# A Mamba-2 scan and a GELU layer on one core: a new order of steps, with the decay products pe on GpSimd and seven filler units fewer

## The chip, the cores and the metric

The kernel runs on one core of a Trainium2 chip. The core has five engines with an instruction queue each: TensorE (PE in the profile; its weight loads are listed as PEld), VectorE (DVE), ScalarE (ACT), GpSimd (POOL) and SyncE (SP), which here only issues DMA transfers. An engine runs its queue strictly in order, so an instruction that waits holds up all that stand behind it. The engines wait for each other by semaphores. The metric is the device time of one launch in microseconds, the median of several runs.

## The reference

The first half is a chunked state-space scan. For each of 4 batches and 8 heads, with 768 tokens of 32 values (x), 16 state values (B, C) and a decay a per token, and with cum the running sum of log a within a chunk:

```python
CB = np.einsum('bhin,bhjn->bhij', Cc, Bc)
M = CB * L                                   # L = exp(cum_i - cum_j), causal
y_intra = np.einsum('bhij,bhjd->bhid', M, xc)
y_inter = np.einsum('bhin,bhnd->bhid', Cc, state) * decay_to_i[:, :, :, None]
y[:, :, sl] = y_intra + y_inter
Bx = np.einsum('bhjn,bhjd->bhjnd', Bc, xc) * decay_from_j[:, :, :, None, None]
state = decay_full[:, :, None, None] * state + np.sum(Bx, axis=2)
```

The second half takes y as 3072 tokens of 256 values through two matrices, `w_in` (256 x 2048) and `w_out` (2048 x 256):

```python
h = x @ w_in
g = 0.5 * h * (1.0 + np.tanh(c * (h + 0.044715 * h * h * h)))
return (g @ w_out).astype(np.float32)
```

## The kernel before, in words

The kernel's chunks have 128 tokens, so a batch has 6. Two chunks of a batch are a unit, and there are 12 units, 0 to 11; units 0 to 2 are batch 0, 3 to 5 batch 1, 6 to 8 batch 2, 9 to 11 batch 3. The work is cut into named steps. A name ends in the unit, chunk or batch that it works on.

**Decays.** `clip` and `R` make running products of a on VectorE; `tp2`, `tp6` turn them and `recip` inverts them. `pe` multiplies the first element of each chunk's clipped a by its running product and spreads the result over a mask, two small products of 128 x 3 and 128 x 48 (L419, L420). `pp` multiplies that on TensorE with a selection matrix, and `pend` copies the result out: the decay of each whole chunk.

**B and C of a batch.** `load_bc.b.i` fetches them (i = 0 is B, 1 is C); `mul.b.i` scales them by the decays into the tile bc16. For batch 1 they are turned on TensorE (`T`, `N`). For batches 2 and 3 they go by way of DRAM: `load_wr.b.i` (L524) writes bc16 to a scratch tensor scr, `load_tr.b.i` (L531) reads it back with a DMA transpose, as ch from C and as bh from B, and `load_bn.b` (L536) reads scr of B once more untransposed. `F.b` (L549) makes ce from ch on VectorE.

**A unit of the scan.** `load_x.u` and `castx.u` bring x of the unit as bf16. `G.u` forms the products of C and B into two PSUM tiles ga, gb (L637, L644); it needs bh and ce of its batch. `M.u.0` and `M.u.1` mask them on VectorE (L654, 1024 columns each). `D.u` forms the state's increment (L679), `S.u.k` updates the state (L750, L752), `SP.c` makes the masked and decayed state of a chunk for the next one (L759). `Y.u` adds up the output; from unit 4 on it is `Yi.u` for the part within chunks (L721) and `YI.u` for the part from the state (L734), and `yev` or `yew` copies it to the tile xm (L348 on ScalarE, L352 on VectorE, L350 on GpSimd: the lines of one helper, `copy`).

**The GELU layer.** `s1.u.i` multiplies `w_in` with xm (units 0 to 3: L790, eight steps of four matmuls; later L795, sixteen steps of two matmuls with 512 columns for two units together, named after the even one). `gelu.u.i` follows on ScalarE (L801, L804). `s2.u.k.q` multiplies with `w_out` (L816, four matmuls), `oev` copies the result out and `store` writes it. `wi` and `wo` cast the weights. All of `s1` and most of `D` and `pp` take turns in the PSUM banks a, b, o and y; a step that takes a bank waits until the bank's last content was copied out.

**Order.** Nothing is scheduled at run time. The string ORDERED lists all steps; the kernel calls them from left to right, and each step appends its instructions to the queue of its engine. So the place of two steps in the string sets their order only if they share an engine. `:A`, `:D`, `:P`, `:S` behind a name pick the engine for steps that may run on several, `@b` picks the PSUM bank. `~51` is filler: matmuls of zeros into bank y, in units of 128 columns, up to four units a matmul (L773).

```python
    def fill(t, n):
        w3 = wz.rearrange("p (o t) -> p o t", o=1)
        for k in range(0, n, 4):
            m = min(4, n - k)
            nc.tensor.matmul(out=t[:, 0:m * 128], lhsT=wz, rhs=w3.to_broadcast([128, m, 128]),
                             start=True, stop=True, skip_group_check=True)
```

Of the kernel before, what the change touches and what calls it, by code (L numbers as in the profile page):

```python
# [11 lines left out]
ALU = mybir.AluOpType  # L12
# [7 lines left out]
c_m16 mulc.0 ~51 tw.1 ew.1.1:A mulc.1 tw.2 mulb c_sub c_unp c_ends ~4 tw.0 peq ew.0.2 ew.0.1 load_wi.1  # L20
ew.0.0:A ew.1.2 c_par ~4 G.0 x4.1 ew.1.0 x4.0:D M.0.0 ~4 ppq GE.2 GE.3 pendq XX.0 ME.2 XD.0 xn.1 ME.3
xn.0:D load_wi.2 SP.0 ~17 Y.0 wi.0.1:A wi.0.0:A S.0.0 clip R S.0.1 yev.0.0.2 wi.1.1 XX.1 XD.1 wi.1.0 tp2
wi.2.1 xn.2 s1.0.0 G.1 S.1.0 s1.0.1 xn.3 gelu.0.0 gelu.0.1 s1.0.2 gelu.0.2 M.1.1 wi.2.0 M.1.0 s1.0.3
gelu.0.3 s1.0.4 s1.0.5 recip1 S.1.1 gelu.0.4 gelu.0.5 SP.1 load_wi.3 wi.3.1 wi.3.0 load_bc1.1 s1.0.6
load_bc1.0 mul1.0:P SP.2 pe mul1.1:P T1.0 bh1:D tp6 Y.1 gelu.0.6 pp load_wo.0 pend:D yev.1.0.2 T1.1 N1
wo.0.0 s1.0.7 load_x.2 ce1.1:D castx.2.None ce1.0:D recip.1 s1.1.0 bn1 SP.3 gelu.0.7 wo.0.1 G.2 D.2
gelu.1.0 S.2.0 s1.1.1 gelu.1.1 s2.0.0.0 s1.1.2 gelu.1.2 s1.1.3 load_bc.1.1 SP.4 load_bc.1.0 M.2.1 M.2.0
gelu.1.3 load_wo.1 s2.0.1.0 mul.1.0 s1.1.4 hold.4 mul.1.1:P recip.2 load_x.3 gelu.1.4 wo.1.0 s1.1.5
wo.1.1 Y.2 gelu.1.5 castx.3.None s1.1.6 yev.2.0.2 T.1.0 s1.1.7 gelu.1.6 load_wo.2 E.1.0 T.1.1 s1.2.0 N.1
gelu.1.7 gelu.2.0 E.1.1 bn.1:D s1.2.1 F.1 s2.0.0.1 wo.2.0 wo.2.1:D s1.2.2 gelu.2.1 s2.0.1.1 D.3 G.3 S.3.0  # L30
gelu.2.2 s1.2.3 gelu.2.3 S.3.1 M.3.0 M.3.1 load_wo.3 load_x.4 wo.3.0:A s2.0.0.2 s2.0.1.2 wo.3.1 SP.6
s1.2.4 s1.2.5 castx.4.None s2.0.0.3 s2.0.1.3 gelu.2.4 gelu.2.5 oev.0:D s1.2.6 load_bc.2.1 load_bc.2.0
# [50 lines left out]
def kernel(  # L83
# [10 lines left out]
    nc = tc.nc  # L94
# [988 lines left out]
```

## Time and profile before

| what | value |
|---|---|
| median of three runs | 116.25 us (115.82 to 116.44) |
| the profiled execution | 115.84 us, span 114.1 us |
| TensorE busy | 107.5 us (94% of the span) |
| VectorE, ScalarE, GpSimd busy | 68.1, 69.7, 24.7 us |
| share of the chain that ended last | PE 78%, SP's queue 9%, DMA 7% |
| filler matmuls (L773) | 21, 7.6 us busy |

The span runs from the first to the last instruction; what the execution takes beyond it, 1.7 us, lies around it. Times in the views are counted from the span's start. The chain is followed back from the last instruction, at each step to what released it, so a share in it says what set the end. A matmul's length in the timeline holds its way through the array: two that follow each other overlap, and their distance is told by their starts. "x4" means that a row stands for four instructions. The engine of a DMA's issue is written SPq; its length there is that of the issue, and the landing is told apart.

### The profile page before, as it was taken

The page shows a single profiled execution, that of the slowest core. Times are in us where ns is not written, and L with a number is a line of the kernel's source. Part 1 is how long each engine was busy: PE and PEld are TensorE (multiplying, and loading weights), DVE is VectorE, ACT ScalarE, POOL GpSimd, SP SyncE. Part 2 cuts the span into 40 slices and gives each one's busy share as a digit, 9 for nine tenths or more (in the row PEclk, how much of TensorE's full clock was granted, in tenths as well). Part 3 has the DMA queues.
Part 4 walks back from the last instruction along what each step waited for, and adds up shares of the span by engine and source line. Part 5 has one row for each costly group of instructions (what it writes and reads, how often), then busy time and mean ns, then how long its engine had stood idle before and what let it go on. Part 6 is the DMA issues. An engine that isn't in the chain of part 4 may idle for free.

```text
span 114.1 us, 3122 instructions
## 1 busy us (share of the span) xinstructions
PE 107.5 (94%) x1277; PEld 77.6 (68%) x1285; DVE 68.1 (60%) x136; ACT 69.7 (61%) x135; POOL 24.7 (22%) x53
## 2 busy tenths in 40 slices
PE   6998889999999999999999999999999999999990
PEld 2345566888879888665677765777657776777870
DVE  4789999999989597798509704658444411020110
ACT  3149688687673727479666778725865666654400
POOL 6635676736319000130200200000000000000000
PEclk9999999999999999999999999999999999999999
DMA  0999989989998768968777502220000023201032
GB/s 24 243 303 306 353 222 203 311 151 345 207 215 136 158 163 188 294 128 195 185 161 142 116 0 96 97 92 6 0 0 0 6 91 116 69 0 52 0 138 92
DMA packets 43102, 15.99 MB, mean 140 GB/s; under 512 B 36688, under 2 KB 41552, under 8 KB 43088
## 3 DMA queue, kind: packets, MB, share of 16 engines
q1 hardware_dynamic: 42896, 15.70, 54.9%
q8 instruction: 10, 0.16, 0.7%
q10 hardware_dynamic: 192, 0.09, 0.3%
q14 instruction: 4, 0.03, 0.1%
HBM read 11.07 MB, written 3.93 MB: 131 GB/s over the span
## 4 chain that ended last, share of the span: by engine, by line
PE 78%; SPq 9%; DMA 7%; ACT 1%; issue 1%; POOL 1%; DVE 0%; POOLq 0%
PE bank_o L816 19%; PE bank_y L816 16%; PE bank_b L795 10%; PE bank_a L795 7%; PE bank_b L790 5%; PE bank_a L790 4%; SPq L154 4%; PE bank_o L795 4%; DMA bcf<-in_B_dram 4%; DMA x_t<-in_x_dram 3%; PE bank_y L795 3%; SPq L194 3%; PE bank_b L816 2%; PE bank_a L816 2%; PE ga L637 1%; PE bank_y L721 1%
## 5 line engine op out<-in xcount | busy, mean ns | idle before, releaser
L816 PEld LDWEIGHTS <-gT 128*128 128x128 bf16 x384 | 37.1, 98 | 10.4 <-issue 0.6
L816 PE MATMUL bank_o<-w_out_sb,gT 128*128 128x256 bf16 x192 | 26.1, 273 | 0.0
L816 PE MATMUL bank_y<-w_out_sb,gT 128*128 128x256 bf16 x160 | 21.2, 273 | 0.1
L795 PEld LDWEIGHTS <-w_in_sb 128*128 128x128 bf16 x128 | 14.1, 114 | 7.7 <-issue 0.4
L804 ACT ACTIVATE gT<-bank_b 128x512 bf16<-128x512 f32 x25 | 14.9, 598 | 6.6 <-PE bank_b L795 6.1
L654 DVE TENSOR_TENSOR m<-ga,tri 128x1024 bf16<-128x1024 f32 x12 | 14.6, 1216 | 5.3 <-PE gb L637 5.3
L804 ACT ACTIVATE gT<-bank_a 128x512 bf16<-128x512 f32 x21 | 12.6, 599 | 6.6 <-PE bank_a L795 2.5
L790 PEld LDWEIGHTS <-w_in_sb 128*128 128x128 bf16 x128 | 13.6, 113 | 2.3 <-issue 1.5
L795 PE MATMUL bank_b<-xm,w_in_sb 128*128 128x512 bf16 x48 | 14.5, 380 | 0.2
L801 ACT ACTIVATE gT<-bank_b 128x512 bf16<-128x512 f32 x17 | 10.1, 596 | 6.8 <-PE bank_b L790 6.7
L654 DVE TENSOR_TENSOR m<-gb,tri 128x1024 bf16<-128x1024 f32 x11 | 13.4, 1216 | 0.1
L352 DVE COPY o_sb<-bank_y 128x256 f32<-128x256 f32 x5 | 2.1, 424 | 15.7 <-PE bank_y L816 13.7
L795 PE MATMUL bank_a<-xm,w_in_sb 128*128 128x512 bf16 x36 | 11.2, 380 | 0.1
L801 ACT ACTIVATE gT<-bank_a 128x512 bf16<-128x512 f32 x15 | 8.9, 595 | 2.7 <-PE bank_a L790 2.6
L790 PE MATMUL bank_b<-xm,w_in_sb 128*128 128x256 bf16 x68 | 10.3, 273 | 0.2 <-DVE s_new L752 0.2
L790 PE MATMUL bank_a<-xm,w_in_sb 128*128 128x256 bf16 x60 | 9.0, 272 | 0.9 <-ACT gT L801 0.4
L759 DVE SCALAR_TENSOR_TENSOR sp_new<-s_new,pend,bmask 128x256 bf16<-128x256 f32 x17 | 9.4, 568 | 0.3 <-DVE s_new L752 0.2
L773 PE MATMUL bank_y<-wz 128*128 128x512 bf16 (+2 forms) x21 | 7.6, 512 | 1.1 <-DVE warm L225 1.1
L352 DVE CAST xm<-bank_a 128x512 bf16<-128x512 f32 x4 | 2.8, 692 | 9.0 <-PE bank_a L734 9.0
L804 ACT ACTIVATE gT<-bank_o 128x512 bf16<-128x512 f32 x10 | 6.0, 596 | 2.4 <-PE bank_o L795 2.3
L510 POOL TENSOR_TENSOR bc<-bc_t,pt 128x768 bf16<-128x768 f32 x3 | 4.5, 1494 | 13.0 <-DMA bc_t<-in_C_dram 10.7
L348 ACT ACTIVATE xm<-bank_y 128x512 bf16<-128x512 f32 x8 | 4.8, 594 | 3.6 <-PE bank_a L734 3.1
(149 smaller groups left out, 131.8 us busy)
## 6 DMA issues: line engine op xcount, KB each, us to landing
out_dram<-o_sb SPq DMA_DIRECT2D x24, 128.0 KB, 1.8
x_t<-in_x_dram SPq DMA_DIRECT2D x20, 128.0 KB, 4.3
wf<-in_moe_w_in_dram SPq DMA_DIRECT2D x4, 512.0 KB, 7.6
wf<-in_moe_w_out_dram SPq DMA_DIRECT2D x4, 512.0 KB, 6.0
bc_t<-in_C_dram SPq DMA_DIRECT2D x3, 384.0 KB, 4.7
bc_t<-in_B_dram SPq DMA_DIRECT2D x3, 384.0 KB, 6.0
scr<-bc SPq DMA_DIRECT2D x4, 192.0 KB, 2.7
x_t<-in_x_dram SPq DMA_DIRECT2D x1, 512.0 KB, 4.5
```

The costliest lines, as they stand in the source:

```text
L154: nc.sync.dma_start(out=BC0[1][:, i], in_=(B, C)[i][0, :, c * Q:(c + n) * Q, :] .rearrange("h (p r) n -> p h (r n)", r=n))
L348: nc.scalar.activation(o, i, AF.Copy)
L352: nc.vector.tensor_copy(out=o, in_=i)
L510: (nc.gpsimd if eng == "POOL" else nc.vector).tensor_tensor(out=d["bc16"][:, i], in0=d["bc"].rearrange("p i h (r n) -> p i r h n", r=R6)[: ...
L654: nc.vector.tensor_tensor(out=m_of(u)[:, 2 * i:2 * i + 2].rearrange("p g k e t -> p (g k e) t"), in0=gx[i].rearrange("p g (k t) -> p (g k) ...
L759: nc.vector.scalar_tensor_tensor(out=sp_new.rearrange("p (g d) -> p g d", g=4), in0=(XN[0][:, H * D:H * D + 64] if gc == 0 else state[("s" ...
L773: nc.tensor.matmul(out=t[:, 0:m * 128], lhsT=wz, rhs=w3.to_broadcast([128, m, 128]), start=True, stop=True, skip_group_check=True)
L790: nc.tensor.matmul(out=hp[:, j * T:(j + 1) * T], lhsT=w_in_k[:, w, q, k], rhs=xm[:, w, u * T:(u + 1) * T], start=(w == 0), stop=(w == 1))
L795: nc.tensor.matmul(out=hp, lhsT=w_in_k[:, w, q, k], rhs=xm[:, w, u * T:u * T + PT], start=(w == 0), stop=(w == 1))
L801: nc.scalar.activation(gts[u][:, 2 * i:2 * i + 2], hp.rearrange("p (j t) -> p j t", j=2), AF.Gelu_apprx_tanh)
L804: nc.scalar.activation(gts[("p", u)][:, i], hp, AF.Gelu_apprx_tanh)
L816: nc.tensor.matmul(out=ops[gc], lhsT=gts[u][:, fi, k * Q:(k + 1) * Q], rhs=w_out_sb[:, fi, :], start=(fi == 0 and (u > 0 or k == 0)), stop ...
```

## The change

There are three parts. The step `pe` takes an engine as argument and now runs on GpSimd; the first filler has 44 units in place of 51; and all steps from the transposed x of unit 1 (`XX.1`) on stand in a new order, some with another engine or bank. Up to there the order is the old one, but that `G.1` and `S.0.1` move into it and `clip` stands later.

```diff
-c_m16 mulc.0 ~51 tw.1 ew.1.1:A mulc.1 tw.2 mulb c_sub c_unp c_ends ~4 tw.0 peq ew.0.2 ew.0.1 load_wi.1
+c_m16 mulc.0 ~44 tw.1 ew.1.1:A mulc.1 tw.2 mulb c_sub c_unp c_ends ~4 tw.0 peq ew.0.2 ew.0.1 load_wi.1
...
-s2.4.0.3 oev.8:A F.3 s1.6.0@a gelu.6.0 s1.6.1@b SP.18 s1.6.2@o s2.4.1.0@y s2.4.1.1 gelu.6.1 s1.6.3@b
...
+s1.4.15@b s2.4.0.0@o M.7.1 s2.4.0.1 gelu.4.14 gelu.4.15 Yi.6@ya D.8@b D.9@y Yi.7 G.8 YI.6 YI.7 S.9.0
+S.9.1 castx.10.None:D yew.6.1 S.8.0 yew.6.0 s2.4.0.2 s2.4.0.3 oev.8:D s1.6.0@a s1.6.1@b gelu.6.1
...
-    def f_pe():
+    def f_pe(eng):
+        ve = nc.gpsimd if eng == "POOL" else nc.vector
         first = [t[:, 0:QL].rearrange("p (c t) -> p c t", t=Q // 2)[:, :, 0] for t in (ac, r_t)]
-        nc.vector.tensor_tensor(out=pe1, in0=first[0], in1=first[1], op=ALU.mult)
-        nc.vector.tensor_tensor(
+        ve.tensor_tensor(out=pe1, in0=first[0], in1=first[1], op=ALU.mult)
+        ve.tensor_tensor(
             out=pe2, in0=pe1.rearrange("p (o c) -> p o c", o=1).to_broadcast([128, 4 * batch, 3]),
             in1=m16.rearrange("p (j o) -> p j o", o=1).to_broadcast([128, 4 * batch, 3]), op=ALU.mult)
...
-    pe_ = add("D", f_pe, deps=[R, cm16])
+    pe_ = add("D", f_pe, alt="DP", deps=[R, cm16])
```

The old order had `Yi.6@ya Yi.7 D.8@b D.9 YI.6 YI.7 G.8 yew.6.1 yew.6.0 S.9.0 s2.4.0.2 S.8.0 S.9.1` ahead of the removed line shown second. Units 8 and 9 go the same way: G.10 stood behind YI.9 and now stands ahead of YI.8. At unit 10, `s2.8.0.2 s2.8.0.3 s2.8.1.0` stood between YI.11 and s1.10.0; now the first two do. Lines of the changed kernel stand one to two further down than those named above.

The first place is SP's queue around the scratch copies of batch 2. Here scr21 is the scratch of C, scr20 that of B; x_t_777 is x of unit 6, x_t_848 of unit 7, x_t_774 of unit 5. Before:

```order
L168 DMA bc_t_771<-in_C_dram 128x8x96
L168 DMA bc_t_771<-in_B_dram 128x8x96
L175 DMA x_t_774<-in_x_dram 128x8x32 x2
L175 DMA x_t_777<-in_x_dram 128x8x32 x2
L524 DMA scr21_842<-bc16_834 128x768
L175 DMA x_t_848<-in_x_dram 128x8x32 x2
L524 DMA scr20_852<-bc16_834 128x768
L531 DMA_TRANSPOSE ch_854<-scr21_842 128x768
L536 DMA bn_857<-scr20_852 128x6x128
L531 DMA_TRANSPOSE bh_865<-scr20_852 128x768
```

Now, with x of units 5, 6 and 7 as x_t_724, x_t_849 and x_t_859:

```order
L176 DMA x_t_724<-in_x_dram 128x8x32 x2
L169 DMA bc_t_750<-in_C_dram 128x8x96
L169 DMA bc_t_750<-in_B_dram 128x8x96
L176 DMA x_t_849<-in_x_dram 128x8x32 x2
L526 DMA scr20_857<-bc16_753 128x768
L176 DMA x_t_859<-in_x_dram 128x8x32 x2
L526 DMA scr21_866<-bc16_753 128x768
L533 DMA_TRANSPOSE ch_876<-scr21_866 128x768
L538 DMA bn_892<-scr20_857 128x6x128
L533 DMA_TRANSPOSE bh_910<-scr20_857 128x768
```

The two copies to scr have changed places, x of unit 5 has moved ahead of B and C of batch 2, and the two transposes stand as before. What the first copy waits for is on VectorE now, where mul.2.0 (bc16_753) follows both M.4 (m_840) and the cast of unit 5:

```order
L353 COPY o_sb_776<-bank_o_145 128x256
L754 SCALAR_TENSOR_TENSOR s_new_821<-s_new_707,pend_129,bank_b_144 128x64
L754 SCALAR_TENSOR_TENSOR s_new_831<-s_new_821,pend_129,bank_b_144 128x64
L353 CAST x16_834<-x_t_724 128x512
L656 TENSOR_TENSOR m_840<-gb_142,tri_112 128x1024
L656 TENSOR_TENSOR m_840<-ga_141,tri_112 128x1024
L512 TENSOR_TENSOR bc16_753<-bc_t_750,rt_126 128x768
```

Before, both products of batch 2 (bc16_834) stood on GpSimd, C's first:

```order
L350 CAST w_out_sb_139<-wf_650 128x512
L350 CAST w_out_sb_139<-wf_728 128x512
L350 CAST x16_753<-x_t_730 128x512
L510 TENSOR_TENSOR bc16_834<-bc_t_771,pt_127 128x768
L510 TENSOR_TENSOR bc16_834<-bc_t_771,rt_126 128x768
L510 TENSOR_TENSOR bc16_918<-bc_t_885,pt_127 128x768
```

C's product of batch 2 stayed there; B's left.

The second place is VectorE ahead of D.2. Before, from recip1 on:

```order
L408 RECIPROCAL pt01_125<-rt01_123 128x16
L752 SCALAR_TENSOR_TENSOR s_new_441<-s_new_409,pendq_128,bank_o_145 128x64
L759 SCALAR_TENSOR_TENSOR sp_new_445<-s_new_344,pendq_128,bmask_111 128x256
L759 SCALAR_TENSOR_TENSOR sp_new_458<-s_new_409,pendq_128,bmask_111 128x256
L419 TENSOR_TENSOR pe1_107<-ac_104,r_t_106 128x3
L420 TENSOR_TENSOR pe2_108<-pe1_107,m16_113 128x48
L352 COPY bh01_135<-ga_141 128x256
L375 STREAM_TRANSPOSE rt_126<-r_t_106 128x192
```

Now, from recip1 to the cast of unit 2 (x16_528):

```order
L409 RECIPROCAL pt01_125<-rt01_123 128x16
L472 TENSOR_TENSOR bc0s1_131<-bcf1_95,pt01_125 128x256
L353 CAST xm_140<-bank_y_146 128x2x2x128
L353 COPY bh01_135<-ga_141 128x256
L376 STREAM_TRANSPOSE rt_126<-r_t_106 128x192
L353 COPY pend_129<-bank_a_143 128x2x4x2
L353 COPY pend_129<-bank_a_143 128x2x4
L353 CAST w_out_sb_139<-wf_492 128x512
L353 CAST x16_528<-x_t_500 128x512
```

The two products of pe are gone from here, and mul1.1, yev.1, a cast of `w_out` and castx.2 have come.

The third place is VectorE at the evacuation of unit 6's xm (yew.6.1, the CAST of xm). Before:

```order
L654 TENSOR_TENSOR m_1205<-gb_142,tri_112 128x1024
L352 CAST xm_140<-bank_a_143 128x512
L750 COPY s_new_1318<-bank_b_144 128x64
L752 SCALAR_TENSOR_TENSOR s_new_1324<-s_new_1111,pend_129,bank_b_144 128x64
L752 SCALAR_TENSOR_TENSOR s_new_1326<-s_new_1318,pend_129,bank_b_144 128x64
```

Now:

```order
L656 TENSOR_TENSOR m_1193<-gb_142,tri_112 128x1024
L752 COPY s_new_1314<-bank_b_144 128x64
L754 SCALAR_TENSOR_TENSOR s_new_1316<-s_new_1314,pend_129,bank_b_144 128x64
L353 CAST x16_1318<-x_t_1130 128x512
L353 CAST xm_140<-bank_a_143 128x512
L754 SCALAR_TENSOR_TENSOR s_new_1321<-s_new_1109,pend_129,bank_b_144 128x64
```

Two updates of the state and the cast of x of unit 10 (x_t_1130) have moved ahead of the evacuation.

More of the change, by code (lines that the diff above doesn't have):

```diff
@@ L23 @@
[L23 to L32, printed above, removed]
@@ new lines @@
+xn.3:A gelu.0.1 pe:P s1.0.2@b s1.0.3@a gelu.0.3 s1.0.4@o gelu.0.4 s1.0.5@a wi.3.0:P load_bc1.1 load_bc1.0
+gelu.0.2 tp2 recip1 wi.3.1:P mul1.1:D Y.1 yev.1.0.2:D s1.0.6@b load_wo.0 T1.1 mul1.0:P gelu.0.5 T1.0
+load_x.2:S pp@a gelu.0.6 bh1:D s1.0.7@o N1 tp6 ce1.1:A pend:D s1.1.0@b wo.0.1:D s1.1.1@y bn1:A gelu.0.7
+ce1.0:A castx.2.None:D recip.1 D.2@o S.2.0 gelu.1.0 G.2 s1.1.2@b gelu.1.1 SP.3 gelu.1.2 load_bc.1.1
+wo.0.0:P SP.4 s1.1.3@y s2.0.0.0@o M.2.1 hold.4 s1.1.4@b gelu.1.3 s2.0.1.0 load_bc.1.0 gelu.1.4 s1.1.5@a
```

75 lines of the change are left out of this document (40 added, 35 removed).

## The prediction

> **What bounds the kernel now.** I read the head of the page first, then the busy time by stretch, then the chain of waits in order of time, and last the timelines where that chain leaves TensorE.
>
> ```profile
> PE 107.5 (94%) x1277; PEld 77.6 (68%) x1285; DVE 68.1 (60%) x136; ACT 69.7 (61%) x135; POOL 24.7 (22%) x53
> ...
> PEclk9999999999999999999999999999999999999999
> ```
> TensorE (PE) bounds the kernel: it is 94% busy, at full granted clock. The stretches (length, then busy us of PE, PEld, DVE, ACT, POOL, then granted clock, DMA share, GB/s) show where it still waits.
>
> ```profile
> 10.90:20.30 9.40, 8.18 (x158) 5.99 (x157) 9.16 (x26) 7.61 (x16) 6.02 (x12) 1.00 1.00 267
> 20.30:45.60 25.30, 25.10 (x344) 21.71 (x348) 22.08 (x36) 16.10 (x31) 9.32 (x11) 1.00 0.90 207
> 45.60:111.00 65.40, 64.98 (x700) 45.70 (x708) 28.98 (x50) 40.47 (x78) 2.72 (x3) 1.00 0.34 87
> ```
> In the first PE idles 1.22 us (9.40 less 8.18) while VectorE and the DMA are full. After 20.30 it idles 0.2 and 0.4 us, beside tails of matmuls that count as busy. So the order of 45.60 to 111 can hardly be made better, only worse; what can be won lies before 45.60. The chain in order of time shows what ends the first stretch:
>
> ```profile
> 15.73 3.83 DMA x_t<-in_x_dram
> ...
> 19.68 0.62 POOL x L350
> ...
> 20.35 0.21 PE bank_b L679 x4
> ```
> x of unit 2 lands at 19.56, GpSimd casts it, and D.2 starts at 20.35.
>
> **The filler.** Timeline, start in us, length, engine:
>
> ```profile
> 1.07 5.41 PE L773 MATMUL bank_y<-wz 128*128 128x512 bf16 x13 [1.07 <-DVE warm L225]
> 6.31 0.39 PE L460 MATMUL bank_a<-ident,cz 128*128 128x128 bf16 x4
> 6.34 0.69 DVE L451 TENSOR_TENSOR bc0s<-bcf,rt 128x512 bf16<-128x512 f32 x1 [0.43 <-DMA bcf<-in_B_dram]
> 7.09 0.40 PE L460 MATMUL bank_o<-ident,bc0s 128*128 128x128 bf16 x4
> 9.93 1.09 PE L773 MATMUL bank_y<-wz 128*128 128x512 bf16 x5
> ```
> 51 units take 6.31 - 1.07 = 5.24 us, so seven take 0.72. I cost their removal at nothing: tw.0 at 7.09 waits for mulb, which waits for B's landing and ends at 7.03. The filler's end moves to 5.6, tw.1 and tw.2 follow it, and PE idles longer ahead of tw.0. If mulb were early, the cut would be worth up to 0.72.
>
> **pe on GpSimd.**
>
> ```profile
> 16.86 0.61 DVE L419 TENSOR_TENSOR pe<-ac,r_t 128x3 f32<-128x3 f32 x1
> 17.50 0.59 DVE L420 TENSOR_TENSOR pe<-pe,m 128x48 f32<-128x48 f32 x1
> 16.77 0.68 POOL L470 TENSOR_TENSOR bc0s<-bcf,rt 128x256 bf16<-128x256 f32 x1 [0.56 <-DMA bcf<-in_B_dram]
> ```
> VectorE gets 0.61 + 0.59 = 1.2 us back. GpSimd has no such small product in the trace: between nothing and two of the 0.68 us products, 1.4 us. I take 0.6, since 48 columns are far from 256. Behind it queue wi.3's two casts and mul1.0, and behind them s1.0.6 and T1.0; GpSimd idles 9.40 - 6.02 = 3.4 us there, so even 1.4 is covered.
>
> **The head up to D.2.** x of unit 2 stands at the same place of SP's queue, behind the same loads, so it lands at 19.56 again. Its cast moves to VectorE:
>
> ```profile
> 42.74 0.42 DVE L352 CAST x<-x_t 128x512 bf16<-128x512 f32 x1
> 21.57 0.44 PE bank_b L790 x4
> ```
> 0.42 for 0.62, so D.2 at about 20.1, 0.25 earlier. s1.1.1 (0.44) now stands ahead of D.2 and G.2 behind it; eight matmuls of a quarter of the rows, four side by side, cost G.2 a little less than an s1, and I credit 0.1. PE has room, with 1.22 us idle in that stretch. VectorE ahead of the cast now has yev.1, wo.0 and mul1.1 in place of pe, ce1 and a product of mask and state, about even. Together 0.35 (0 if VectorE comes late to the cast, 0.5 at most). The waits of PE between 20.3 and 45.6 shrink as well: G.4, Y.3 and s1.2.7 stand in another order there. That adds 0.2 (0 to 0.5, the small gaps that the timeline shows in that stretch, tails set aside). So PE comes to G.6 at 45.60 - 0.55 = 45.05.
>
> **G.6 and the transposes of batch 2.** This term decides. G.6 needs bh, which the last of a chain on SP's queue brings. SP's issues, and issue to landing of the two copies to scr, ch and bh:
>
> ```profile
> 35.73 0.67 SPq L524 DMA_DIRECT2D scr<-bc  x1
> 36.45 2.26 SPq L175 DMA_DIRECT2D x_t<-in_x_dram  x2
> 38.81 0.89 SPq L524 DMA_DIRECT2D scr<-bc  x1
> 40.13 1.23 SPq L531 DMA_TRANSPOSE ch<-scr  x1
> 41.59 0.39 SPq L536 DMA_DIRECT2D bn<-scr  x1
> 42.03 1.23 SPq L531 DMA_TRANSPOSE bh<-scr  x1
> ```
> ```profile
> scr<-bc SPq DMA_DIRECT2D x1, 192.0 KB, 4.4
> ```
> ```profile
> scr<-bc SPq DMA_DIRECT2D x1, 192.0 KB, 2.7
> ```
> ```profile
> ch<-scr SPq DMA_TRANSPOSE x1, 2.7
> ```
> ```profile
> bh<-scr SPq DMA_TRANSPOSE x1, 3.2
> ```
> ```profile
> 45.60 0.29 PE L637 MATMUL ga<-ce,bh 32*64 32x256 bf16 x1
> ```
> Now the copy that lands first (35.73 + 4.4 = 40.1) is the one that the ch transpose needs, so this goes at 40.13 while the second copy is still under way (38.81 + 2.7 = 41.5). bh lands at 42.03 + 3.2 = 45.2, 0.4 ahead of G.6. The change swaps the copies: scr20 is issued first, scr21, which the ch transpose needs, last, behind x of unit 7; and all three reads of scr follow. No transpose can start before both copies have landed. scr20's product, mul.2.0, also moves, from GpSimd to VectorE, behind both products of M.4:
>
> ```profile
> 35.60 1.68 POOL L510 TENSOR_TENSOR bc<-bc_t,rt 128x768 bf16<-128x768 f32 x1
> 33.41 0.28 DVE L752 SCALAR_TENSOR_TENSOR s_new<-s_new,pend,bank_b 128x64 f32<-128x64 f32 x1 [0.21 <-PE bank_b L679]
> 36.98 1.21 DVE L654 TENSOR_TENSOR m<-ga,tri 128x1024 bf16<-128x1024 f32 x1
> 51.04 0.95 DVE L510 TENSOR_TENSOR bc<-bc_t,rt 128x768 bf16<-128x768 f32 x1
> ```
> S.4.0 starts at 33.4 less up to 0.5 of gain, 33.1; S.4.0 and S.4.1 0.56, the cast 0.42, M.4 2.42, mul.2.0 0.95: 37.4 (37.0 to 37.8). SP, which now issues its first copy at 35.73, stands until then, and x of unit 7 behind it. From there to the second copy's landing: at most as now, 41.5 - 35.73 = 5.8, since x of unit 6 still clogs the queue today; at least 0.67 for the first issue, 0.9 for two unclogged x (half of today's 2.26 is 1.1) and 2.0 for a copy that finds the queue empty (today's second takes 2.7; both are estimates), 3.6. I take 3.9, near the low end, as the queue drains during the wait: 41.3. The ch transpose and bn take 42.03 - 40.13 = 1.9 less the 0.2 that bn waited: 1.7. bh then needs 2.7 to 3.2: landing 46.2 (45.0 to 48.3). G.6 at 46.2 is 0.6 later than now, and what the head gained is spent in this wait. In its shadow lies what else stands behind SP's wait: ch lands at 41.4 + 2.7 = 44.1 and VectorE's F.2 follows it before 45; x of unit 7 lands a little ahead of the second copy, near 41, and holds up gelu.3.5 behind its cast on ScalarE by some tenths, which PE would otherwise wait away at G.6.
>
> **Units 6, 8 and 10.** From the last state products YI to the first s1 of the next pair, the evacuations of xm must fit.
>
> ```profile
> 45.65 0.22 PE L734 MATMUL bank_y<-ch,sp_new 32*64 32x128 bf16 x2
> 46.08 0.69 DVE L352 CAST xm<-bank_a 128x512 bf16<-128x512 f32 x1 [1.13 <-PE bank_a L734]
> 46.83 0.41 PE L795 MATMUL bank_a<-xm,w_in_sb 128*128 128x512 bf16 x1
> 90.64 0.22 PE L734 MATMUL bank_y<-ch,sp_new 32*64 32x128 bf16 x2
> 90.85 1.05 PE L816 MATMUL bank_o<-w_out_sb,gT 128*128 128x256 bf16 x8
> ```
> That takes 46.83 - 45.65 = 1.18. Cover after the change at units 6 and 8: G is moved ahead of YI, so two s2 steps are left, (90.85 - 90.64) + 2 x 0.44 = 1.09, a wait of 0.1 each; at unit 10 two s2 in place of three, again 0.1. Bounds: 0 and 0.2 each. At unit 4 such a wait of 0.1 exists now and goes, since G.6 comes late. Together +0.2. Stores, gelu order and the tail: the last eight s2 steps and one evacuation end both programs, nothing.
>
> **Sum.** 0 (filler) + 0 (pe) + 0.6 (G.6, head gain included) + 0.2 = 0.8 us. The profiled execution took 115.84, 0.41 under the median 116.25 of the three runs (115.82 to 116.44); so 116.6 on its own scale, 117.0 on the median's.
>
> **Rivals.** (1) The transposes land in time and the head's gain stays. For it: TensorE could be up to 0.4 + 0.5 early, at 44.7; the copies need 192 KB each on a queue that idles while SP waits. Against: the lowest sum of the rows gives 45.0. It decides at a second landing of 40.0 or earlier. Time: -0.9 + 0.3 for the covers = -0.6, 115.6. (2) The chain lands at 45.0 to 45.7, G.6 where it is now: 116.3. (3) Batch 3 waits too. x of unit 10, now cast on VectorE ahead of the evacuation of unit 6's xm, follows bn of batch 3 on the queue:
>
> ```profile
> 57.74 1.20 SPq L175 DMA_DIRECT2D x_t<-in_x_dram  x2
> x_t<-in_x_dram SPq DMA_DIRECT2D x1, 128.0 KB, 4.7
> ```
> It is issued at 57.74 now and takes 4.7; issued at 55.8 as I place it, it lands at 60.5, and the cast is due at 60.0. Such a wait adds 0.5 to 1: 117.9. (4) The clock. From 1.07 to 6.31 a filler of 512 columns takes 0.41 us, at 9.93 0.26 (1.09 over 17 units): PE runs at little more than half rate until 6.3, though the granted clock above reads full. With seven units fewer the full rate could come later. If it came 3.4 us later, the PE work of that time would take up to 1.7 us more, of which the 1.22 us of idle hides most: +0.5, 117.5. The Trainium skill, TensorE: Matmul & The Clock Gate, Part 1, has the rate doubled after a busy window of about 3.4 us that runs free of the kernel's start; by that rule busy work that is cut can miss a window. Against it here: tw.1, tw.2 and four units follow the filler without a gap.
>
> **How the numbers follow.** Forecast (transposes late, 116.4 to 117.8 with the bounds of its terms) 0.45; (1) 0.18; (2) 0.20; (3) 0.12; (4) 0.05. Half a per cent, 0.58 us, is about what runs of this kernel tell from no change. Faster is (1), 0.18. Within are (2) and the low edge of the forecast, 0.26. Slower is the rest, 0.56. A range of 115.7 to 118.2 leaves out most of (1) and the tail of (3).
>
> **What would show it.** In the trace after: PE idle ahead of G.6 at 45 to 46.2 with bh's landing as its end; no transpose before 41; mul.2.0 on VectorE ending near 37.4; D.2 near 20.1; gaps of 0.1 ahead of the first s1 of units 6, 8, 10. I am wrong if G.6 starts by 45, or if PE does not wait there at all.

## The result: slower by 3%, with one wait at G.6

The changed kernel takes 120.31 us (median of four runs, 118.93 to 121.2), the kernel before beside it 116.03 (115.77 to 116.44). The ratio is 1.0325, with a 95% interval of 1.022 to 1.043. Measured again later with six executions it was 119.98 against 116.27, a ratio of 1.0196 [1.0116, 1.0276]. Ratios here and below use the executions that the comparison counted as undisturbed; since a clock that falls behind a wait is counted as a disturbance too, medians over all executions stand beside them.

The head of the page of the changed kernel (span 118.1 us, 119.9 for the execution):

```profile
PE 106.9 (91%) x1283; PEld 77.1 (65%) x1283; DVE 66.2 (56%) x134; ACT 72.9 (62%) x142; POOL 21.0 (18%) x48
```

TensorE's share falls from 94% to 91%. The stretches of the changed kernel, with the columns as before (length, busy time of PE, PEld, DVE, ACT, POOL, granted clock, DMA share, GB/s):

```profile
10.90:20.30 9.40, 7.78 (x154) 6.17 (x152) 9.12 (x24) 7.72 (x16) 5.03 (x10) 1.00 0.93 254
20.30:45.60 25.30, 24.43 (x312) 20.96 (x310) 19.96 (x34) 18.34 (x37) 5.58 (x7) 1.00 0.83 188
45.60:49.10 3.50, 1.17 (x54) 0.72 (x52) 1.68 (x4) 1.05 (x2) 0.00 (x0) 1.00 0.86 185
49.10:111.00 61.90, 61.90 (x661) 42.59 (x662) 27.25 (x47) 39.68 (x75) 3.74 (x3) 1.00 0.37 88
```

Ahead of 45.60 TensorE idles 0.4 and 0.7 us more than before. Between 45.60 and 49.10 it works 1.17 of 3.50 us. Behind 49.10 it has no gap. The list of waits names the cause (time, times, longest):

```profile
PEld L639 <- DMA bh<-scr: 2.5, 1, 2.5
```

It is G.6, for bh of batch 2, the place that the prediction named. TensorE's own row has it at 49.09, with 2.33 us of idle time ahead (its weight loads waited 2.5):

```profile
49.09 0.29 PE L639 MATMUL ga<-ce,bh 32*64 32x256 bf16 x2 [2.33 <-DMA bh<-scr]
```

The chain of waits in order of time shows how bh came to land at 49.05, where it had landed at 45.23:

```profile
31.36 1.98 SPq L169
33.39 5.00 DMA bc_t<-in_B_dram
38.41 0.97 DVE bc L512
...
41.19 2.86 DMA scr<-bc
44.06 1.23 SPq L533
45.39 0.52 SPq L538
45.97 3.08 DMA bh<-scr
```

B of batch 2 is issued at 33.39 and lands at 38.39; only then can VectorE form its product. SP has stood since 36.5 and issues its first copy at 39.40, x of unit 7, and at 41.19 the second copy, which lands at 44.04. The three reads follow.

The 3.92 us between the two profiled spans (118.05 less 114.135) split into: TensorE comes to the end of YI.5 0.83 later (46.48 for 45.65); the step from there to G.6 takes 2.61 for 0.08, 2.53 more; from G.6 to the last s2 step it needs 0.20 more (64.90 for 64.70); and behind that step's start the program ends 0.36 later. (Before, G.6 runs into the end of YI.5; the split takes its row at 45.73. From its earliest row, 45.60, the work behind G.6 differs by 0.07 and the step by 2.66.)

### The profile page after: what moved, and what is told of

Read it like the earlier page. It is cut to its first block, busy times and chain, and to the rows that moved or that the text cites. A ratio compares the mean times of both kernels' runs of the same rounds, so it can differ in the third digit from the quotient of the medians.

```text
span 118.1 us, 3123 instructions
## 1 busy us (share of the span) xinstructions
PE 106.9 (91%) x1283; PEld 77.1 (65%) x1283; DVE 66.2 (56%) x134; ACT 72.9 (62%) x142; POOL 21.0 (18%) x48
## 4 chain that ended last, share of the span: by engine, by line
PE 55%; SPq 26%; DMA 13%; issue 1%; DVE 1%; ACT 0%
PE bank_y L818 13%; PE bank_o L818 13%; PE bank_b L797 9%; SPq L176 9%; PE bank_a L797 8%; SPq L195 7%; DMA bc_t<-in_B_dram 4%; SPq L155 4%; PE bank_o L797 4%; DMA bcf<-in_B_dram 4%; SPq L169 3%; PE bank_y L797 3%; DMA bh<-scr 3%; DMA scr<-bc 2%; PE ga L639 2%; PE bank_a L818 1%
## 5 line engine op out<-in xcount | busy, mean ns | idle before, releaser
L818 PE MATMUL bank_y<-w_out_sb,gT 128*128 128x256 bf16 x176 | 23.5, 273 | 0.0
L806 ACT ACTIVATE gT<-bank_b 128x512 bf16<-128x512 f32 x25 | 14.9, 596 | 8.3 <-PE bank_b L797 7.7
L806 ACT ACTIVATE gT<-bank_a 128x512 bf16<-128x512 f32 x21 | 12.5, 596 | 2.9 <-PE bank_a L797 2.8
L797 PE MATMUL bank_a<-xm,w_in_sb 128*128 128x512 bf16 x42 | 12.6, 382 | 0.0
L803 ACT ACTIVATE gT<-bank_b 128x512 bf16<-128x512 f32 x15 | 9.0, 597 | 1.9 <-PE bank_b L792 1.9
L792 PE MATMUL bank_b<-xm,w_in_sb 128*128 128x256 bf16 x60 | 9.0, 272 | 0.7 <-ACT gT L803 0.4
L761 DVE SCALAR_TENSOR_TENSOR sp_new<-s_new,pend,bmask 128x256 bf16<-128x256 f32 x17 | 8.2, 504 | 0.3 <-issue 0.2
L353 DVE COPY o_sb<-bank_y 128x256 f32<-128x256 f32 x3 | 1.3, 425 | 12.3 <-PE bank_y L818 9.3
L775 PE MATMUL bank_y<-wz 128*128 128x512 bf16 (+1 forms) x19 | 6.1, 458 | 1.1 <-DVE warm L226 1.1
L349 ACT ACTIVATE o_sb<-bank_y 128x256 f32<-128x256 f32 x8 | 3.1, 384 | 5.8 <-PE bank_y L818 4.4
L803 ACT ACTIVATE gT<-bank_a 128x512 bf16<-128x512 f32 x10 | 6.0, 598 | 0.6 <-PE bank_a L792 0.6
L792 PE MATMUL bank_a<-xm,w_in_sb 128*128 128x256 bf16 x40 | 6.1, 274 | 0.0
```

Source lines behind the costliest of these rows:

```text
L349: nc.scalar.activation(o, i, AF.Copy)
L761: nc.vector.scalar_tensor_tensor(out=sp_new.rearrange("p (g d) -> p g d", g=4), in0=(XN[0][:, H * D:H * D + 64] if gc == 0 else state[("s" ...
L792: nc.tensor.matmul(out=hp[:, j * T:(j + 1) * T], lhsT=w_in_k[:, w, q, k], rhs=xm[:, w, u * T:(u + 1) * T], start=(w == 0), stop=(w == 1))
L797: nc.tensor.matmul(out=hp, lhsT=w_in_k[:, w, q, k], rhs=xm[:, w, u * T:u * T + PT], start=(w == 0), stop=(w == 1))
L803: nc.scalar.activation(gts[u][:, 2 * i:2 * i + 2], hp.rearrange("p (j t) -> p j t", j=2), AF.Gelu_apprx_tanh)
L806: nc.scalar.activation(gts[("p", u)][:, i], hp, AF.Gelu_apprx_tanh)
```

## The experiments

### Which part of the chain counts

Four kernels undo pieces of the change in the handling of batch 2, each with all else as in the changed kernel. First, the copies alone, C's ahead again:

```diff
-load_x.6:S s1.3.1@a gelu.3.0 load_wr.2.0:S load_x.7:S s2.1.0.2 load_wr.2.1:A
+load_x.6:S s1.3.1@a gelu.3.0 load_wr.2.1:S load_x.7:S s2.1.0.2 load_wr.2.0:S
```

> The changed kernel with only the two copies to scr swapped back: C's copy (scr21) first, B's behind x of unit 7. Theory (the chain of the transposes of batch 2 sets G.6): C's copy can go at about 38.5, when its product on GpSimd has ended, B's follows its product (39.4) at about 39.8 to 40.5 and lands at 43; the ch transpose no longer waits for the last copy, so bn and bh go 1.9 earlier than now relative to the last landing: bh at about 46.5 to 47.5 in place of 49.05, G.6 about 2 us earlier, 118.3 on the scale of the changed kernel's 120.3. Rival (the wait at G.6 is only where lost time shows, the loss comes from the head's loads landing late): bh earlier, but the time within 0.6 of 120.3.

Measured: 117.75 (117.06 to 121.11) beside 116.61, ratio 1.0098 [1.0057, 1.0138]. The wait for bh is nearly gone:

```profile
PE ga L639 <- DMA bh<-scr: 0.3, 1, 0.3
```

The copies' order alone is worth some 2.5 us here, with the clock that is told below. With C's copy first, the ch transpose is issued at 41.23, while B's copy (issued at 40.48) is still under way, and bh lands 3.5 behind the last copy, not 5.0.

Second, B's product back on GpSimd:

```diff
-mul.2.1:P ... M.4.0 gelu.2.7 mul.2.0:D load_x.6:S
+mul.2.1:P mul.2.0:P ... M.4.0 gelu.2.7 load_x.6:S
```

> The changed kernel with only B's product of batch 2 (mul.2.0) back on GpSimd, behind C's. Theory (what holds the product is B's landing at 38.4, not its engine): GpSimd needs 1.68 where VectorE needs 0.96, from the same landing on, so the first copy goes 0.7 later, at 40.1, and the kernel is 0.7 slower than the changed one, 121.0. Rival (as forecast: the product is late because it stands behind M.4 on VectorE): it ends at 37.4 or earlier and the kernel gains 1 to 2 us, about 118.8.

Measured: 119.85 (118.86 to 121.19) beside 116.61, ratio 1.0189 [1.0129, 1.0248]: against 1.0325 and 1.0196 for the changed kernel itself, no loss and no gain that these runs can tell. B landed at 37.82 there, 0.6 earlier than in the first profile, and the product follows it on GpSimd:

```profile
37.89 1.58 POOL bc L512
...
41.09 2.79 DMA scr<-bc
```

The first copy goes at 39.49, where it went at 39.40. So the engine of the product is not the cause: in both profiles it starts only when B has landed.

Third, x of unit 5 back behind B and C:

```diff
-load_x.4:S gelu.2.2 load_x.5:S ... load_bc.2.1 load_bc.2.0 mul.2.1:P
+load_x.4:S gelu.2.2 ... load_bc.2.1 load_bc.2.0 load_x.5:S mul.2.1:P
```

> The changed kernel with only x of unit 5 back behind the loads of B and C of batch 2. Theory: B lands about 2.4 us earlier, near 36, the product then follows M.4 on VectorE and ends near 38.2 in place of 39.4, all that follows moves by 1.2, G.6 at 47.9, time 119.1. If B's landing doesn't matter, no gain, 120.3. If the cast of unit 5 (ahead of M.4 on VectorE) waits for its later x, the product comes as late as before and again nothing is gained.

Measured: 122.5 (122.03 to 122.54), ratio 1.0483 [1.044, 1.0527], the slowest of all. It is the third of the three cases expected, and worse than put there:

```profile
32.70 4.32 DMA x_t<-in_x_dram
37.47 2.26 DVE m L656 x2
39.73 0.88 DVE bc L512
```

B lands at 36.02, but on VectorE the cast of unit 5 stands ahead of M.4, and its x lands at 37.02. M.4 and the product go behind it, and the first copy at 40.62. All four executions also have a fallen clock, 0.981 to 0.986. The earlier x of unit 5 is what the new place of its cast needs; the two moves belong together.

Fourth, all three undone at once:

```diff
-load_x.5:S ... load_bc.2.1 load_bc.2.0 mul.2.1:P ... mul.2.0:D load_x.6:S ... load_wr.2.0:S load_x.7:S ... load_wr.2.1:A
+load_bc.2.1 load_bc.2.0 load_x.5:S mul.2.1:P mul.2.0:P ... load_x.6:S ... load_wr.2.1:S load_x.7:S ... load_wr.2.0:S
```

> The changed kernel with all three undone: copies, product and x of unit 5 as in the kernel before. Theory: no wait at G.6 longer than some tenths; the 2.5 us that TensorE waits there in the changed kernel come back, 117.8, and what is left against 116.0 is the 1.0 that TensorE comes later to this place and 0.5 behind it. Rival (the head decides: since loads of the head land 1.5 us late, the chain is late with it): the wait stays above 1 us and the time above 119.

Measured: 117.87 (116.57 to 121.21, eight executions), 1.0087 [1.004, 1.0134]: as much as the copies alone. In the profiled execution, the longest of the eight, x of units 0 and 1 landed at 11.01 in place of 8.4, the granted clock was 0.50 from 10.5 to 17.3, all ran 4 us late, and TensorE did not wait for bh at all, from 50.12 (YI.5) to 50.20 (G.6).

### The same pieces put into the kernel before

The whole chain, with the order of units and the head as before:

```diff
-load_bc.2.1 load_bc.2.0 load_x.5 ... mul.2.1:P ... load_wr.2.1 load_x.7 mul.2.0:P load_wr.2.0
+load_x.5 load_bc.2.1 load_bc.2.0 ... mul.2.1:P ... castx.5.None:D M.4.1 M.4.0 mul.2.0:D load_wr.2.0 load_x.7 load_wr.2.1
```

> The kernel before with the change's handling of batch 2 alone: x of unit 5 ahead of its B and C, B's product on VectorE behind the cast of unit 5 and both products of M.4, the two copies swapped. Theory: B lands near 37, its product ends near 38.2, the last copy lands 4.6 later at 42.8, bh 5.0 later at 47.8, G.6 waits 2.2 from 45.6 on: 118.2 at full clock and up to 1 us more where the granted clock falls to a half behind the wait. Rival (the chain matters only since the changed head delays the loads): bh by 46, time within 0.6 of 116.0.

Measured: 119.94 (118.36 to 121.99) beside 116.77. The wait:

```profile
PE ga L636 <- DMA bh<-scr: 1.8, 1, 1.8
```

B landed at 37.07, the last copy at 42.93, bh at 48.01, each within 0.3 of what was expected. So by the medians this piece makes 3.2 of the 4 us without the changed head; three of its four executions have a mean clock of 0.986, the one at 0.997 took 118.36.

The two copies swapped alone, both products on GpSimd:

```diff
-mul.2.1:P ... load_wr.2.1 s2.1.0.1 load_x.7 mul.2.0:P load_wr.2.0 load_tr.2.1
+mul.2.1:P ... s2.1.0.1 mul.2.0:P load_wr.2.0 load_x.7 load_wr.2.1 load_tr.2.1
```

> The kernel before with the two copies swapped alone: B's copy first, behind B's product on GpSimd, which ends at 37.2; x of unit 7; then C's copy, and the three reads. Theory (no read of scr can start before both copies have landed): first copy at 37.3 in place of 35.7, last landing 1.6 later less what the emptier queue gives, near 42.0, then 4.9 to 5.0 as in the changed kernel: bh at 46.9, G.6 1.2 later, 118.0 beside 116.8 of the kernel before. Rival (what counts is only when a copy is issued): ch lands as before and G.6 moves by no more than 0.3, 117.0.

Measured: 117.71 (117.15 to 118.11) beside 116.46, ratio 1.01 [1.0013, 1.0188].

```profile
38.51 0.70 SPq L174
39.26 2.74 DMA scr<-bc
42.01 1.23 SPq L530
43.35 0.52 SPq L535
43.92 3.06 DMA bh<-scr
```

First copy at 37.63, second landing at 42.00, bh at 46.98, G.6 at 47.03: 1.4 later than the 45.60 before, where 1.2 was worked out. In the changed kernel the same swap is worth 2.5, since the chain is later there. A read of scr that is queued behind both copies costs even where nothing else is moved.

### The other parts, each alone

The tail: the kernel before up to D.7, the changed order behind it, with the steps that either part lacks put in at the seam:

```diff
-D.7 yew.4.1 s2.2.1.3 oev.5:D yew.4.0 s1.4.0@a S.6.0 ...
+D.7 yew.4.1 s2.2.1.3 mul.3.0:P yew.4.0 s1.4.0@a s2.3.0.0@y load_wr.3.0:S ...
```

> The kernel before up to D.7, the changed order from there on (units 4 to 10, batch 3, stores, end). Theory by the two traces: TensorE takes 0.2 longer from G.6 to its end (as forecast for the covers), and 0.35 to 0.45 more come between the end of TensorE's work and the end of the execution: 116.6. Rival (batch 3 waits with x of unit 10 cast on VectorE): a gap ahead of the first s1 of unit 6, 117.0 or more. If the tail is worth nothing: 116.0.

Measured: 117.2 beside 116.77, ratio 1.0045 [1.0007, 1.0082]. TensorE needs 0.67 more from G.6 to the last s2 (65.37 for 64.70), about 0.4 of it at G.7, which is explained below. No gap stands ahead of the first s1 of unit 6, so x of unit 10 is in time. But the 0.36 at the program's end, which had been put down to this part, isn't there (below).

pe on GpSimd and the filler of 44:

```diff
-c_m16 mulc.0 ~51 ... pe mul1.1:P
+c_m16 mulc.0 ~44 ... pe:P mul1.1:P
```

> The kernel before with the two products of pe on GpSimd and the first filler of 44 units, and nothing else. As forecast both cost nothing: 116.0, between 115.7 and 116.4. Rivals: the shorter filler lets the full clock come later, 116.5; or the products on GpSimd hold up wi.3's casts and with them s1.0.6, 116.5.

Measured: 116.61 beside 116.77, ratio 1.001 [0.9974, 1.0047]. Both cost and gain nothing, together. On GpSimd the two products took, in the changed kernel:

```profile
15.35 0.19 POOL L421 TENSOR_TENSOR pe<-ac,r_t 128x3 f32<-128x3 f32 x1
15.62 0.27 POOL L422 TENSOR_TENSOR pe<-pe,m 128x48 f32<-128x48 f32 x1
```

0.46 for the pair, where 0.6 had been taken. The head up to D.2, everything behind it as before:

```diff
-D.2 gelu.1.0 S.2.0 s1.1.1 gelu.1.1 s2.0.0.0
+D.2@o wo.0.0 SP.3 G.2 gelu.1.0 S.2.0 gelu.1.1 s2.0.0.0
```

> The changed kernel up to D.2, the order of the kernel before from there on. The trace of the changed kernel has D.2 at 20.65 in place of 20.35, with s1.1.1 (0.44) already done: by that a loss of 0 to 0.2 is all that this part makes, 116.0 to 116.2 in place of the gain of 0.35 that was forecast. Rival (the loads of the head land up to 1.5 later under the changed order, and what follows them waits): T.1.0 waits for B of batch 1 and the time is 117 or more.

Measured: 116.77 beside 116.77, ratio 1.0029 [0.9985, 1.0073], D.2 at 20.71. And the middle, from D.2 to G.6, with batch 2 as before:

```diff
-D.2 gelu.1.0 S.2.0 s1.1.1 ... G.4 gelu.2.6 D.4 Y.3 ...
+D.2 s1.1.1@y S.2.0 gelu.1.0 ... G.4 Y.3 oev.0:A D.4@b S.4.0 ...
```

> The kernel before up to D.2 and from G.6 on; between them the changed order, with copies, product and x of unit 5 of batch 2 as before. By subtraction (copies swapped back leave 1.1; 0.2 of it is TensorE's work after G.6, 0.35 the end of the program) 0.3 to 0.6 must lie here: 117.1 to 117.4 beside 116.8 of the kernel before. As forecast this part gains 0.2: 116.6.

Measured: 116.37 beside 116.46, ratio 0.9953 [0.9913, 0.9992], the only one that came out ahead. It was measured again:

> The kernel before up to D.2 and from G.6 on, between them the changed order with copies, product and x of unit 5 of batch 2 as before: once more with more executions. If its gain is real, 0.5 below the kernel before (ratio 0.995); if the first time was chance, within 0.3% of it.

Measured: 116.42 beside 116.27, ratio 1.0025 [0.9984, 1.0067]. The gain was not repeated. Head and middle are worth nothing that these runs can tell, and no variant beats the kernel before.

### The clock behind the wait

The profiled execution of the changed kernel shows the full clock, others of it don't: their mean granted clocks are 1.000, 0.982, 0.997 and 0.986. Where the profile caught an execution with a lower clock, the stretches show it. The changed kernel again (YI.5 ends at 45.99, G.6 starts at 48.02; the column behind the five engines is the granted clock):

```profile
48.00:49.00 1.00, 0.98 (x36) 0.69 (x37) 0.19 (x1) 0.00 (x0) 0.00 (x0) 1.00 1.11 290
49.00:50.00 1.00, 0.78 (x5) 0.47 (x4) 0.89 (x5) 0.38 (x1) 0.00 (x0) 0.55 1.18 283
50.00:51.00 1.00, 1.00 (x5) 0.61 (x5) 1.00 (x1) 0.60 (x1) 0.00 (x0) 0.50 1.23 268
51.00:52.00 1.00, 1.00 (x5) 0.47 (x4) 1.00 (x4) 0.20 (x1) 0.00 (x0) 0.50 0.80 133
52.00:53.00 1.00, 1.00 (x6) 0.65 (x5) 1.00 (x2) 0.40 (x1) 0.72 (x1) 0.74 0.56 87
```

A good 1 us after the work resumes, the clock is halved, from 49.1 to 52.5. 0.45 + 0.50 + 0.50 + 0.26 = 1.7 us of work are lost by it. In the five profiles with such a stretch TensorE takes 66.6 to 66.9 us from G.6 to its last matmul, in those at full clock that don't wait at G.7 65.0 to 65.3. To see whether the idle time causes it, ten matmuls of zeros were put into the wait, into the bank that G.6 overwrites:

```diff
-Yi.5 YI.4 YI.5 G.6 D.6@b
+Yi.5 YI.4 YI.5 ^40 G.6 D.6@b        # fill(gx[0][:, 0], 40)
```

> The changed kernel with 40 units of filler (ten matmuls of zeros, some 2.3 us) between YI.5 and G.6, into the bank that G.6 then overwrites, so that TensorE works through the wait for bh instead of idling. Theory (the idle time of 2.5 us itself lets the granted clock fall to a half behind it in most executions, as the records of the runs with product and x of unit 5 put back show from 49 to 52 us): the clock stays at 1.00, the wait stays as long as it is, and the median falls from 120.3 to 119.0 to 119.6. Rival (the clock falls for another reason, or costs nothing): no change beyond 0.3, clock records below 0.99 as before.

Measured: 120.23 (119.31 and 119.33, 121.14 and 121.22), clocks 1.00, 1.00, 1.00 and 0.997. The clock stays up as expected, the median does not fall. In the profiled execution, at 121.14 one of the two longer ones, bh itself is late:

```profile
44.75 4.56 DMA bh<-scr
```

4.56 from issue to landing, where 3.08 was seen in the changed kernel; behind the filler TensorE still idled 1.1 us. A second loss lies at G.7, which waited 0.7 for M.6.1. VectorE and GpSimd at that time:

```profile
52.37 3.13 DVE L761 SCALAR_TENSOR_TENSOR sp_new<-s_new,pend,bmask 128x256 bf16<-128x256 f32 x2
55.42 1.21 DVE L656 TENSOR_TENSOR m<-gb,tri 128x1024 bf16<-128x1024 f32 x1
...
52.09 1.49 POOL L512 TENSOR_TENSOR bc<-bc_t,pt 128x768 bf16<-128x768 f32 x1 [15.15 <-DMA bc_t<-in_C_dram]
53.54 1.68 POOL L512 TENSOR_TENSOR bc<-bc_t,rt 128x768 bf16<-128x768 f32 x1
```

Two sp_new take 3.13 us, as long as GpSimd's two products of batch 3 beside them, where alone one takes 0.48. So M.6.1 was moved ahead of them, with the filler and without:

```diff
-M.6.0 SP.14 load_tr.3.1 SP.13 gelu.4.3 M.6.1 s1.4.4@o
+M.6.0 M.6.1 SP.14 load_tr.3.1 SP.13 gelu.4.3 s1.4.4@o
```

> The changed kernel with the wait filled by ten matmuls and M.6.1 moved on VectorE ahead of the two products of state and mask (sp_new of chunks 14 and 13). Theory (two causes of the spread: the halved clock, gone with the filler, and sp_new held up while GpSimd's two products of batch 3 run, which makes M.6.1 and G.7 late): neither is left, all executions lie near 119.3 beside 116.4 of the kernel before, a ratio of 1.024 with a spread under 1 us. Rival (the executions near 121.2 of the filled version have another cause, such as loads that land late): they are still there.

> The changed kernel with M.6.1 ahead of the two sp_new, without the filler. Theory: the halved clock stays in about half of the executions (records near 0.985, 1.6 us longer), those with the full clock lie at 119.0 to 119.6; median 119.5 to 120.5. Rival: if the clock costs nothing, the executions with records below 0.99 lie within 0.5 of the others.

> The changed kernel once more, unaltered, beside the two: 120.3 as before, between 118.9 and 121.3, with clock records between 0.98 and 1.00; the slowest executions have both the halved clock and a late M.6.1.

Measured, in the order of these three: 120.8 (119.0 to 121.57, clocks 0.995 to 1.00), 120.39 (119.61 to 122.3, five of six clocks at 0.986 or lower) and 119.98 (118.12 to 122.65). With M.6.1 first G.7 no longer waits, since M is not held up by GpSimd's product beside it:

```profile
53.60 1.22 DVE L656 TENSOR_TENSOR m<-gb,tri 128x1024 bf16<-128x1024 f32 x1
54.73 2.51 DVE L761 SCALAR_TENSOR_TENSOR sp_new<-s_new,pend,bmask 128x256 bf16<-128x256 f32 x3
```

But the filled version still splits into 119.1 and 121, so the rival is right: the longer executions have another cause. In the profiled one bh again took 4.50 us from issue to landing, and TensorE idled 1.5 us behind the filler.

What can be said of the clock: of 28 executions of the five kernels that wait 1.8 to 2.3 us at G.6, 19 had a mean clock of 0.986 or less; of the ten with the wait filled, none had (lowest 0.995); of the four with a wait of 1.0 (the copies swapped alone), none. Of the 158 executions of all the kernels with a shorter wait or none, the kernel before among them, nine had. In the changed kernel measured again the three at full clock took 118.12, 118.27 and 119.47, the others 120.49, 120.5 and 122.65. So the idle time lets the clock fall, in two executions of three, and by the traces this costs 1.4 to 1.7 us. The filler shows the first half of that only: it kept the clock up and did not shorten the program.

The clock records in the traces also show what the chance hangs on. The clock changes only on a grid of 3.41 us, and the grid lies elsewhere in each execution. In the five profiles with a halved stretch behind G.6, 1.84 to 2.30 us of idle time fell into one window of the grid, and the halving fills the next window (above: window from 45.70 to 49.11, 2.04 idle, then 0.50 to 52.52). In the first profile, whose wait of 2.33 is as long as any, the grid has an edge at 48.22: 1.46 us lie ahead of it and 0.87 behind, and the clock stays. If one window must hold 1.7 us of the wait, a value between these rows, and the wait is 2.1, this is so for (3.41 + 2.1 - 2 x 1.7) / 3.41 = 0.62 of the places that the grid can take, an estimate, beside the 19 of 28. The limit is not sharp: at the program's end windows with 1.90 and 1.95 us of idle time were not followed by a halving.

The late bh is another matter. Its transpose took 4.5 us in both profiles with the filler and 2.8 to 3.7 in the sixteen others. The list of DMA transfers shows what is special in these two: a transfer of 16 KB of instructions lies inside the transpose, from 46.99 in the one and from 48.33 in the other, for 1.1 to 1.2 us. In the changed kernel it begins at 51.85, behind bh's landing. Of all 72 transposes in the eighteen traces, 45 without such a transfer beside them took 2.6 to 3.7 us (median 3.1), and 15 with a whole one of 16 KB inside 3.4 to 5.1 (median 4.4). It fits that the filler's matmuls, more instructions ahead of G.6, bring the transfer forward; this was not tried, and no trace of a filled execution of 119 us was taken.

### The end of the program

In the changed kernel 1.31 us pass from the last store's landing to the end, before 0.95. The records show where: 0.38 us between a DRAIN on GpSimd and its next instruction, a clearing of semaphores, otherwise 0.03. All traces with 72 or 73 records on GpSimd lost 0.35 to 0.5 us behind the last landing, at this place or just ahead of the DRAIN; none with 79 to 85 did. Ten memsets of one column were appended on GpSimd near 85 us to the changed kernel with the copies swapped back:

```diff
-M.10.0 s1.8.4@y
+M.10.0 ^pad s1.8.4@y        # for _ in range(10): nc.gpsimd.memset(padt, 0.0)
```

> The changed kernel with the copies swapped back, and ten memsets of one column on GpSimd near 85 us, where it has nothing to do. Every trace with 72 or 73 instruction records on GpSimd ends 0.35 later behind the last landing than those with 79 or more, with a gap of 0.38 ahead of GpSimd's last clearing of semaphores or a late drain. Theory (a fetch of instructions falls there or not by their count): with 82 the gap is 0.03 and the time 0.35 lower than with the copies alone swapped back, 117.4. Rival (the gap belongs to the order of the stores): the gap stays, 117.75.

Measured: the gap is 0.03, the last landing is 0.95 ahead of the end, and the time is 116.75 beside 116.46, ratio 1.0067 [1.003, 1.0104], where without the memsets it was 1.0098. The profile shows that ten more instructions take the delay away; the ratios fit 0.36 us, though their intervals overlap. That a fetch of instructions lies behind it is argued only; in the changed kernel's trace no transfer of instructions falls into the gap, from 117.27 to 117.65.

## Why the prediction was wrong

**The mechanism held, its size did not.** The prediction had G.6 wait for bh behind SP's late copies, and it does. It put G.6 at 46.2; it started at 49.09, 2.9 later. The step that failed most is the time of the first copy, 2.0 of these 2.9; the way from there to the second landing makes 0.7 and the reads 0.2. A fall of the clock behind the wait was not in the sum at all. The bounds failed with them: the prediction's own latest landing of bh, 48.3, gives 116.25 + 2.7 + 0.2 = 119.2, yet its range ended at 118.2.

**The head.** "So PE comes to G.6 at 45.60 - 0.55 = 45.05" was 0.6 to 1.5 too early: YI.5, which started at 45.65 before, came at 46.48 in the first profile and at 45.69 to 46.57 in seven others with this head (47.5 with x of unit 5 put back, 50.1 where the head's loads came late). It did not set G.6, for which bh came later still. D.2 came at 20.26 to 21.09 in ten profiles, instead of at 20.1. Two credits failed. In the first profile x of unit 2 landed at 19.85, not 19.56, and on VectorE its cast stood behind one of `w_out`, from 20.08 to 20.50; D.2 followed at 20.65, when its bank, now o, came free. And the waits between 20.3 and 45.6 didn't shrink: T.1.0 waited 0.55 for the product of B of batch 1, whose load landed at 25.31, and in five other profiles G.3 waited some 0.3 for ce. The middle alone gave nothing.

**The first copy.** Forecast 37.4, measured 39.40. "S.4.0 starts at 33.4 less up to 0.5 of gain" overlooked that Y.3 now stands ahead of D.4, so that D.4 starts 0.67 behind G.4 and no longer 0.32; with TensorE 1.05 late at G.4, S.4.0 came at 34.82. Then the product waited 0.4 more for B:

```profile
34.82 0.60 DVE L754 SCALAR_TENSOR_TENSOR s_new<-s_new,pend,bank_b 128x64 f32<-128x64 f32 x2 [0.52 <-PE bank_b L681]
38.41 0.96 DVE L512 TENSOR_TENSOR bc<-bc_t,rt 128x768 bf16<-128x768 f32 x1 [0.40 <-DMA bc_t<-in_B_dram]
```

B's landing, which x of unit 5 pushes back on SP's queue, was not in the sum: the move stands in the order of SP that was shown, and only the copies behind it were priced. In the profile of the repeated run B landed at 37.23 and M.4 ended at 37.24, so there both set the product's start.

**From the first copy to the last landing.** "I take 3.9, near the low end": it was 4.64 (39.40 to 44.04), 4.53 when repeated and 4.37 with the copies swapped alone. The first copy, which found the queue empty, took 2.0 as estimated; but the one that counts is the second, behind x of unit 7, and took 2.85, and SP needed 1.79 to come to it, not 1.57.

**The reads.** ch and bn 1.91 for 1.7, bh 3.08 for 2.7 to 3.2: nearly right.

**What was missing altogether** is the clock. The prediction cited the Trainium skill, TensorE: Matmul & The Clock Gate, Part 1, for the filler alone; that part also has the clock fall after an idle window of about 3.4 us. The traces agree with the halving and have it last 3.41 us, but here 1.84 to 2.30 us of idle time in one window were enough, and 19 of 28 executions with such a wait show it. The wait that was forecast, from 45.05 to 46.2, is 1.15 us, and by these rows (1.0 in none of four, 1.46 in one window without effect) would not have set it off. Rival 4 had the right quantity in the wrong place.

**Behind G.6** 0.2 was forecast and 0.20 measured (0.07 from G.6's earliest row), but that is luck: the gaps of 0.1 that were to make it are not there, no wait stands ahead of the first s1 of units 6, 8 and 10. Missing was the 0.36 at the end of the program.

**Right:** nothing for the filler and for pe, measured together; and x of unit 10 (rival 3) was in time. Rivals 1 and 2 fell with the landing at 44.04.

The sum from the runs, beside the kernel before, if the pieces add: the chain 3.2 with its clock, tail 0.4, end of the program 0.35, head and middle 0 to 0.3; together about 4.

## What to carry to other kernels

When a product or copy is moved on a queue that runs in order, work out the start of the moved step from every queue that feeds it (the load's issue, the engine's own order, the transfer) and take the latest of them. Two copies and three reads on one queue cost least when the copy that the first read needs goes first. A wait that grows to 2 us on TensorE is to be priced with the clock that it may lose, not by its length alone. Where a range is given, it should reach as far as the bounds of the term that decides.

## What the runs showed of the hardware that was not expected

- An idle time of 1.8 to 2.3 us on TensorE let the granted clock fall to a half for 3.41 us in 19 of 28 executions; 1.0 us did so in none of four. The clock changes on a grid of 3.41 us, and 2.33 us that an edge of it cut into 1.46 and 0.87 left the clock full.
- A transfer of 16 KB of instructions inside a DMA transpose of 128x768 goes with 3.4 to 5.1 us from issue to landing, against 2.6 to 3.7 without.
- A product on GpSimd holds up sp_new on VectorE. In the kernel before, already:

```profile
34.15 1.49 POOL L510 TENSOR_TENSOR bc<-bc_t,pt 128x768 bf16<-128x768 f32 x1 [2.29 <-DVE s_new L752]
35.60 1.68 POOL L510 TENSOR_TENSOR bc<-bc_t,rt 128x768 bf16<-128x768 f32 x1
...
34.19 1.73 DVE L759 SCALAR_TENSOR_TENSOR sp_new<-s_new,pend,bmask 128x256 bf16<-128x256 f32 x1
```

  1.73 us, until GpSimd's first product is over, for an instruction whose median without such a product is 0.48 in 322 records of the eighteen traces. M, with one operand in PSUM, takes 1.22 either way. The same holds for the price of pe that the prediction read: its 0.61 and 0.59 us on VectorE stand beside two products of GpSimd, and where its product of 128x3 began ahead of these, in two other profiles, it took 0.15 and 0.16. The Trainium skill, Advanced Engine Details and Errata, Miscellaneous Facts (GPSIMD Details), has GpSimd share an interface with VectorE and conflict with its instructions of two SBUF inputs; the trace agrees.
- Ten more instructions on GpSimd moved the program's end by 0.36 us.
- The same loads of the head, in the same order on SP's queue, land up to 2.4 us apart between profiles: B of batch 1 at 22.95 to 25.31, and at 23.9 to 25.3 among those with the changed head.
